# One word list for another: a linear-attention and ReLU² kernel with all of its engine orders, transfers and banks rewritten

## The chip, the cores and the metric

The kernel runs on one core of a Trainium2 chip. The metric is device microseconds of one execution; the median of three runs before the change is 180.9 us (180.63 to 181.43). Five engines work side by side: PE (matmuls; its weight loads are listed apart as PEld), DVE (vector), ACT (activations and copies), POOL (a second elementwise engine) and SP, which here issues every transfer. Each engine takes its own instructions strictly in the order in which the program gives them; between engines, semaphores make an instruction wait for what it reads, or for the buffer that it overwrites.

## The reference

Two stages, for 4 batches, 8 heads, 768 positions and 48 channels to a head:

```python
for t in range(S):                                  # attention, a state of 48x48 per head
    cur = einsum('bhd,bhe->bhde', u * k_t, v_t)
    y_t = einsum('bhd,bhde->bhe', r_t, state + cur)
    state = w_t[..., None] * state + einsum('bhd,bhe->bhde', k_t, v_t)
x = y.transpose(0, 2, 1, 3).reshape(3072, 384)      # tokens x (heads * channels)
out = (maximum(x @ w_in, 0) ** 2) @ w_out           # 384 -> 2048 -> 384
```

r, k, v and w are float32, 4.7 MB each; w_in and w_out 3.1 MB each; the output is 4.7 MB.

## The kernel before, in words

The 3072 tokens are cut into 12 **steps** of 256 tokens, three to a batch. A step of the attention is done in chunks: logarithms of w are summed with a matmul (`cum_`), their exponentials scale r and k (`rd_`), products of r and k give a masked score matrix (`p_`, masked by `pm_`), which times v gives `y_`; the state of the chunk before enters through `yc_`, and the state is carried on by `su_` (a matmul), `ts_` (its sum with the old state) and `sn_` (its decay, on POOL). The result (`ysb_`, which also adds `vq_`, the u term) is turned (`yt_` and `xt_` through PE in steps 0 to 5, `dyt_` by a transposing transfer in steps 6 to 11) and goes into the second stage: `m1_.s.g` is one of 8 groups of the first product of step s (six matmuls), `rl_` its ReLU, `sq_` the square of two groups, `m2_.s.c.q` a quarter of the second product of half a step (four matmuls), `os_` scales it into an output tile, `store` sends it out. r and k of steps 0 to 3 are turned on PE (`tr_`, copied by `rkt_`), those of steps 4 to 11 by transposing transfers (`dtr_`).

The order of all this is a **word list**, ORDER: 865 words, each one operation. A loop at the end of the kernel takes them one by one and emits their instructions, so each engine's program is the list read with the other engines' words left out. `ld.3.k` loads k of step 3, `ld.1.i` a quarter of w_in, `ld.1.o` one of w_out; `=V`, `=A`, `=G` puts an operation on DVE, ACT or POOL; `:0` to `:3`, `:m`, `:b` give the PSUM bank. `warm_.8.5` is eight matmuls on zeros whose result nobody reads, there to keep PE going. Nothing but this list decides what stands behind what.

Buffers tie words together as well: four buffers for each of the raw inputs w, k, r, v, four staging buffers for the two weights, two for most tiles of the attention, three of `gt` (the values between the two products), four of the output. A transfer on SP's queue that has to wait, for a tile or for a buffer, holds up every transfer after it in the list.

Of the kernel before, what the change touches and what calls it, by code (L numbers as in the profile page):

```python
# [27 lines left out]
qp_.2=G pm_.2.1 pm_.2.0 su_.2:1 rl_.1.1=V ts_.2.0=V ld.2.i m1_.0.0:2 m1_.1.3:1 cast.i.2=A y_.2:1 q_.2 yc_.2.0
sn_.2.0 yc_.2.1 rl_.1.3=A m1_.0.5:3 ld.3.i m1_.1.5:1 ld.3.w m1_.0.4:0 rl_.0.0=A rl_.0.5=V qs_.2=A rl_.1.5=A
cast.i.3=G m1_.1.7:3 ld.0.o m1_.1.4:1 vq_.2=V ysb_.2=V rl_.0.4=A rl_.1.7=A ww_.3=G cast.o.0=G m1_.0.7:2 yt_.2:3  # L30
ld.2.o m1_.0.6:0 lw_.3 cast.o.2=G cum_.3:1 xt_.2=V rl_.0.7=V ld.3.o m1_.2.4:3 rl_.0.6=V sq_.0.1=A ld.1.o
sq_.0.0=A rl_.1.4=A m1_.2.2:2 sq_.0.2=A m1_.1.6:0 m1_.2.7:1 ld.3.r rl_.1.6=A sq_.1.1=A rl_.2.2=V rl_.2.4=V
m1_.2.5:2 rl_.2.7=V ld.3.k al_.3 rl_.2.5=V cast.o.1=V m1_.2.6:0 m2_.0.1.0:3 m2_.0.1.2 sq_.1.3=V kw_.3=G
m1_.2.3:1 sq_.1.0=A ld.3.v ld.5.w m2_.0.0.0:2 ac_.3 ld.4.w ld.4.r sq_.0.3=A rl_.2.6=A exp_.3 vs_.3.1=G ld.4.v
ld.4.k m1_.2.0:0 m2_.0.0.2 m2_.0.1.1 cast.o.3=V rl_.2.0=A m1_.2.1:0 rw_.3=V m2_.0.1.3 sq_.2.3=A rl_.2.1=A
sq_.1.2=A rl_.2.3=A rd_.3.0 m2_.0.0.1 os_.0.1=A tr_.3.0:0 rd_.3.1 m2_.0.0.3 tr_.3.1:1 ku_.3=V m2_.1.0.1:3
os_.0.0=A m2_.1.0.0 rkt_.3.0=V rkt_.3.1=V p_.3.0:0 v_.3=G sq_.2.1=A su_.3:1 sq_.2.2=A vs_.3.0=A qp_.3=V ld.5.k
p_.3.1:b ts_.3.0=A m2_.2.0.1:2 m2_.1.0.3 m2_.2.0.3 m2_.1.0.2 sq_.2.0=A ww_.4=G pm_.3.0 lw_.4 q_.3 qs_.3=A
cum_.4:0 m2_.2.0.0 ld.6.w v_.4=A pm_.3.1 ww_.5=G rw_.4=G sn_.3.0 ts_.3.1=V vq_.3=G ac_.4 al_.4 m2_.2.0.2
yc_.3.1:1 y_.3 m2_.2.1.0:1 m2_.2.1.2 os_.1.0=A kw_.4=V lw_.5 ysb_.3=V sn_.3.1 store.0.0 os_.2.0=A exp_.4 kw_.5=G  # L40
rd_.4.1 rd_.4.0 cum_.5:1 ac_.5 yt_.3:3 vs_.4.1=G xt_.3=A ld.5.r vs_.4.0=A al_.5 store.0.1 ld.6.r m2_.2.1.3
m2_.2.1.1 os_.2.1=V m1_.3.0:3 rl_.3.0=A exp_.5 su_.4:0 m1_.3.1:2 rl_.3.1=A m2_.1.1.3:0 m2_.1.1.1 dtr_.4.1
ku_.4=V qp_.4=V rw_.5=V m1_.3.7:2 rl_.3.7=A m1_.3.6:1 ts_.4.0=V dtr_.4.0 rl_.3.6=A m2_.1.1.2 m1_.3.5:3 rd_.5.1
rl_.3.5=A m1_.3.4:1 sn_.4.0 ts_.4.1=V p_.4.0:0 q_.4 rd_.5.0 qs_.4=A ww_.6=G vq_.4=G rw_.6=G p_.4.1:1 sq_.3.0=V
m2_.3.1.0:3 m2_.1.1.0 pm_.4.0 yc_.4.1:0 yc_.4.0 sq_.3.3=A m1_.3.3:2 rl_.3.4=A sq_.3.2=A pm_.4.1 y_.4 lw_.6
m1_.3.2:1 rl_.3.3=A rl_.3.2=A cum_.6:1 m2_.3.0.2:2 m2_.3.0.3 sq_.3.1=A m2_.3.1.3 m2_.3.1.1 ku_.5=G qp_.5=G
ld.5.v ysb_.4=V al_.6 ld.7.w ld.6.k ww_.7=G yt_.4:1 m2_.3.1.2 m2_.3.0.0 exp_.6 ac_.6 os_.1.1=V sn_.4.1 m2_.3.0.1
kw_.6=V rd_.6.0 rd_.6.1 dtr_.5.1 ld.6.v v_.5=G dtr_.5.0 xt_.4=A p_.5.1:1 store.2.0 ld.7.r vs_.5.1=A os_.3.1=A
lw_.7 su_.5:b p_.5.0:0 q_.5 v_.6=A store.2.1 ts_.5.0=V m1_.4.1:1 ku_.6=G rl_.4.1=A vs_.6.0=A m1_.4.3:0 os_.3.0=A
pm_.5.0 pm_.5.1 rl_.4.3=V m1_.4.2:3 rl_.4.2=A vs_.6.1=A qs_.5=G m1_.4.4:1 sn_.5.0 yc_.5.1:0 yc_.5.0 rl_.4.4=V  # L50
su_.6:1 dtr_.6.0 m1_.4.7:3 rl_.4.7=A vs_.5.0=G dtr_.6.1 y_.5 m1_.4.6:1 ts_.6.0=V sn_.6.0 ld.9.w m1_.4.5:3
m1_.4.0:2 vq_.5=V sq_.4.1=A rl_.4.6=A rl_.4.5=A sq_.4.2=A ysb_.5=V ts_.6.1=V rl_.4.0=V sq_.4.0=V yt_.5:0
m2_.4.1.1:1 xt_.5=A qp_.6=G q_.6 qs_.6=G ld.7.k p_.6.0:1 ld.8.v yc_.6.1:0 ld.7.v ld.8.r p_.6.1:m store.1.1
ld.8.w vq_.6=G ku_.7=G pm_.6.1 sq_.4.3=A kw_.7=G m2_.4.1.0 m2_.4.1.2 m1_.5.1:0 rl_.5.1=A pm_.6.0 m2_.4.1.3
sn_.6.1 m1_.5.0:2 cum_.7:1 y_.6 m1_.5.7:3 vs_.7.0=A rl_.5.0=A os_.4.1=A ww_.9=V al_.7 m2_.4.0.0:0 rl_.5.7=V
m1_.5.2:2 m1_.5.6:1 ww_.8=G rw_.7=G exp_.7 ac_.7 m2_.4.0.1 vs_.7.1=G m2_.4.0.2 m1_.5.3:3 rl_.5.2=A sq_.5.0=A
v_.7=A rl_.5.3=A m1_.5.5:2 sq_.5.1=A ysb_.6=V vs_.8.0=G m2_.4.0.3 lw_.8 rl_.5.6=A rd_.7.1 qp_.7=V rd_.7.0
sq_.5.3=A su_.7:0 v_.8=G rl_.5.5=V rw_.8=V m1_.5.4:3 rl_.5.4=V m2_.5.1.0:2 cum_.8:1 sq_.5.2=A ts_.7.0=V al_.8
q_.7 m2_.5.1.1 m2_.5.1.3 store.1.0 ld.8.k ld.11.k ac_.8 store.3.1 dyt_.6 dtr_.7.1 dtr_.7.0 exp_.8 kw_.8=V
sn_.7.0 ts_.7.1=V m1_.6.2:3 m2_.5.1.2 m1_.6.3:1 ld.9.r ld.10.w sn_.7.1 os_.4.0=A rd_.8.1 m1_.6.1:0 os_.5.1=A  # L60
ku_.8=G m1_.6.7:2 rd_.8.0 rl_.6.2=V ld.9.k rl_.6.3=A qs_.7=A m1_.6.4:1 su_.8:1 rl_.6.7=A p_.7.1:m p_.7.0:0
qp_.8=G rl_.6.1=V ts_.8.0=V yc_.7.1:1 yc_.7.0 rl_.6.4=A sq_.6.1=A m2_.5.0.2:0 m1_.6.6:1 store.3.0 rl_.6.6=A
sq_.6.3=A dtr_.8.1 pm_.7.1 pm_.7.0 lw_.9 dtr_.8.0 m2_.5.0.1 m1_.6.5:2 y_.7 m1_.6.0:3 m2_.5.0.3 m2_.5.0.0
store.4.1 ku_.9=G q_.8 qs_.8=G ww_.10=G rl_.6.5=V vq_.7=V rl_.6.0=A vs_.8.1=A rw_.9=G sq_.6.0=A p_.8.0:m
p_.8.1:0 kw_.9=G qp_.9=G ysb_.7=V cum_.9:1 m2_.6.0.1:1 ld.9.v ld.10.k os_.5.0=A m2_.6.0.3 m2_.6.1.3:0 m2_.6.0.0
sq_.6.2=V m2_.6.0.2 m2_.6.1.0 sn_.8.0 al_.9 exp_.9 pm_.8.0 rd_.9.0 pm_.8.1 dyt_.7 v_.9=A ac_.9 m1_.7.7:2 y_.8:0
yc_.8.1 rd_.9.1 su_.9:1 vs_.9.1=A yc_.8.0 rl_.7.7=A m1_.7.4:3 ld.10.v vq_.8=G ysb_.8=V m1_.7.0:2 lw_.10
store.4.0 q_.9 rl_.7.4=A ts_.9.0=A rl_.7.0=A cum_.10:0 al_.10 vs_.9.0=V exp_.10 m2_.6.1.1 os_.6.0=V m2_.6.1.2
os_.6.1=A m1_.7.5:2 m1_.7.6:3 m1_.7.2:0 kw_.10=G ld.11.w dtr_.9.0 kw_.11=V qs_.9=G rl_.7.5=A ld.10.r dyt_.8
sq_.7.2=A m1_.7.3:2 m1_.7.1:1 rl_.7.6=A dtr_.9.1 m1_.8.5:3 rl_.7.3=A rl_.7.1=A m1_.8.6:2 v_.10=G sn_.9.0  # L70
ts_.9.1=V rw_.10=G rd_.10.1 rd_.10.0 ac_.10 ku_.11=G rl_.7.2=A rl_.8.5=V sq_.7.1=A ld.11.v m1_.8.7:1 p_.9.0:1
p_.9.1:0 m1_.8.1:3 ww_.11=G store.6.1 vq_.9=G ld.11.r vs_.10.1=G store.6.0 pm_.9.0 sn_.9.1 rl_.8.6=A rl_.8.7=A
rl_.8.1=A lw_.11 m2_.7.1.2:0 m2_.7.1.1 pm_.9.1 m1_.8.3:2 y_.9:0 yc_.9.1 su_.10:1 ysb_.9=V dtr_.10.0 m1_.8.4:1
sq_.7.3=A sq_.7.0=A cum_.11:0 m2_.7.1.3 m2_.7.1.0 ts_.10.0=V rw_.11=V rl_.8.4=A rl_.8.3=V dtr_.10.1 ku_.10=G
sq_.8.2=A os_.7.1=A m1_.8.0:1 m2_.7.0.0:3 m2_.8.1.2:2 m1_.8.2:0 m2_.7.0.1 m2_.7.0.3 m2_.7.0.2 al_.11 exp_.11
rd_.11.1 rd_.11.0 vs_.11.1=G v_.11=G ac_.11 rl_.8.0=A sq_.8.0=A yc_.10.0:0 rl_.8.2=V qp_.10=G p_.10.1:b sn_.10.0
vs_.10.0=G ts_.10.1=V q_.10 qs_.10=G store.7.1 dyt_.9 yc_.10.1 p_.10.0:1 m2_.8.1.0 pm_.10.0 qp_.11=G sn_.10.1
# [555 lines left out]
```

## Time and profile before

| what | value |
|---|---|
| median of 3 runs | 180.9 us |
| lowest, highest | 180.63, 181.43 us |
| profiled execution, first to last instruction (span) | 178.8 us |
| between that span and the median of the runs | 2.1 us |
| PE busy | 171.0 us, 96% of the span |
| DVE, ACT, POOL busy | 138.0, 133.4, 108.0 us |
| bytes moved by the transfers | 35.81 MB |
| first matmul of the second stage (`m1_`) | at 26.02 us |

The profile gives the profiled execution no time of its own beside its span, so what lies around the span is taken as the difference to the median, 2.1 us. Times in what follows are us from the start of the span. A busy time of PE counts matmuls from their start to their modelled end, and these overlap: rows of the chain of waits, which have starts that follow each other, tell more of PE's pace than a mean duration does.

### The profile page before, as it was taken

How to read it: one execution, taken by the hardware profiler on the slowest of the kernel's cores; microseconds unless marked ns; L12 is line 12 of the kernel's file. 1: busy time of each engine (PE TensorE's matmuls, PEld its weight loads, DVE VectorE, ACT ScalarE, POOL GpSimd, SP SyncE). 2: the span in 40 equal slices, each digit the busy share in tenths (PEclk: the TensorE clock that was granted, in tenths of full speed). 3: DMA queues.
4: the chain of work that ended last, by engine and by line, in shares of the span. 5: the costliest groups of instructions: out<-in, count | busy, mean ns of one | idle time of the engine just before them, and what ended most of it. 6: DMA issues, size and time to landing. Idle time of an engine off the chain costs nothing.

```text
span 178.8 us, 5697 instructions
## 1 busy us (share of the span) xinstructions
PE 171.0 (96%) x2383; PEld 123.9 (69%) x2385; DVE 138.0 (77%) x204; ACT 133.4 (75%) x238; POOL 108.0 (60%) x132
## 2 busy tenths in 40 slices
...
GB/s 144 268 263 252 259 346 361 344 368 260 266 243 237 191 216 185 290 166 259 273 291 151 213 255 224 222 175 245 226 79 148 55 48 40 127 12 88 88 44 88
DMA packets 78952, 35.81 MB, mean 200 GB/s; under 512 B 72144, under 2 KB 77392, under 8 KB 78928
## 3 DMA queue, kind: packets, MB, share of 16 engines
...
q8 instruction: 18, 0.29, 0.7%
...
## 4 chain that ended last, share of the span: by engine, by line
PE 56%; POOL 16%; DMA 10%; DVE 9%; issue 4%; SPq 3%; ACT 1%; POOLq 0%; ACTq 0%; DVEq 0%
PE m L562 16%; PE bk L534 11%; PE m L534 11%; PE bk L562 10%; DMA k_raw<-in_k_dram 7%; POOL ku L297 3%; DMA kT<-kdec_buf 3%; POOL r_raw L286 2%; SPq L178 2%; POOL ku L302 2%; DVE pmT L432 2%; PE att L418 2%; POOL ku L316 2%; POOL S L459 2%; DVE y_sb L502 2%
## 5 line engine op out<-in xcount | busy, mean ns | idle before, releaser
L534 PEld LDWEIGHTS <-wi_sb 128*128 128x128 bf16 x576 | 54.9, 98 | 10.7 <-ACT wi_sb L200 0.6
L562 PEld LDWEIGHTS <-gt 128*128 128x128 bf16 x384 | 36.7, 98 | 20.6
L534 PE MATMUL m<-xT,wi_sb 128*128 128x256 bf16 x306 | 40.2, 273 | 0.1
L551 ACT ACTIVATE gt<-gt 128x1024 bf16<-128x1024 f16 x37 | 38.1, 1051 | 0.5
L534 PE MATMUL bk<-xT,wi_sb 128*128 128x256 bf16 x270 | 35.8, 273 | 0.4 <-ACT wi_sb L200 0.4
L562 PE MATMUL bk<-wo_sb,gt 128*128 128x384 bf16 x192 | 35.6, 326 | 0.0
L562 PE MATMUL m<-wo_sb,gt 128*128 128x384 bf16 x192 | 35.0, 326 | 0.0
L543 ACT ACTIVATE gt<-m 128x512 f16<-128x512 f32 x33 | 19.4, 595 | 11.5 <-PE m L534 11.2
L543 ACT ACTIVATE gt<-bk 128x512 f16<-128x512 f32 x35 | 20.6, 596 | 7.2 <-PE bk L534 6.9
L545 DVE TENSOR_SCALAR gt<-m 128x512 f16<-128x512 f32 x18 | 12.3, 688 | 13.1 <-PE m L534 12.4
L432 DVE TENSOR_TENSOR pmT<-att,mask 128x1024 bf16<-128x1024 f32 x16 | 19.1, 1218 | 1.9 <-PE att L418 1.8
L316 POOL TENSOR_TENSOR ku<-v_sh,qs 128x768 f32<-128x768 bf16 x9 | 13.3, 1475 | 10.6 <-ACT qs L277 10.5
L459 POOL TENSOR_TENSOR S<-t_state,ac_buf 128x192 bf16<-128x192 f32 x20 | 12.2, 610 | 8.2 <-DVE t_state L454 5.5
L297 POOL TENSOR_TENSOR ku<-k_raw,u_bc 128x768 f32<-128x768 f32 x9 | 16.7, 1854 | 0.2 <-DMA k_raw<-in_k_dram 0.2
L502 DVE TENSOR_TENSOR y_sb<-att,ku 128x768 bf16<-128x768 f32 x12 | 11.5, 955 | 4.4 <-POOL ku L316 2.0
L290 POOL TENSOR_TENSOR k_raw<-k_raw,w_raw 128x384 f32<-128x384 f32 x8 | 8.1, 1012 | 10.9 <-DMA k_raw<-in_k_dram 10.9
L361 DVE TENSOR_TENSOR kdec_buf<-k_raw,att 128x768 bf16<-128x768 f32 x12 | 11.4, 950 | 3.7 <-ACT att L340 3.7
L277 ACT CAST v_sh<-v_raw 64x384 bf16<-64x384 f32 x26 | 13.2, 509 | 0.3
L302 POOL TENSOR_TENSOR ku<-ku,r_raw 128x768 f32<-128x768 f32 x7 | 12.7, 1811 | 0.2
L358 DVE TENSOR_TENSOR rdec_buf<-r_raw,att 128x384 bf16<-128x384 f32 x24 | 12.3, 547 | 0.6 <-POOL r_raw L286 0.4
L277 POOL CAST v_sh<-v_raw 64x384 bf16<-64x384 f32 x18 | 10.0, 556 | 3.3 <-DMA v_raw<-in_v_dram 2.0
L307 DVE TENSOR_REDUCE q<-ku 128x16 f32<-128x768 f32 x12 | 11.3, 944 | 0.0
...
## 6 DMA issues: line engine op xcount, KB each, us to landing
...
```

Source lines behind the costliest of these rows:

```text
L277: copy(out[j * Q:(j + 1) * Q, c], src[c * Q:(c + 1) * Q, :, j])
L297: tensor_mul("ku_", s, h)(tiles["ku", s][:, hs], raw["k", s][:, hs, 1:3, :], u_bc[:, hs, None, :].to_broadcast([C, n, 2, D]))
L302: tensor_mul("qp_", s, h)(ku, ku, raw["r", s][:, heads(h), 0:2, :])
L316: tensor_mul("vq_", s)(vq[:], tiles["vs", s][:], tiles["qs", s][:, :, :, None].to_broadcast([C, 2, H, D]))
L358: nc.vector.tensor_mul(rdec[0][:, ps, j, :, 0:D], x[:, :, j, :].rearrange("p (a e) d -> p a e d", e=2), dec.rearrange("p (a e) d -> p a e ...
L432: nc.vector.tensor_mul(pmT, ps_p[:].rearrange("p e (x t) -> p (e x) t", t=C), mk.to_broadcast([C, 8, C]))
L459: nc.gpsimd.tensor_mul(t[:], tiles.pop(("ts", s, c))[:].rearrange("p (a d) -> p a d", a=HP), tiles["a_c", s][:, :, c, None].to_broadcast([ ...
L502: nc.vector.tensor_add(tiles["ysb", s][:, x].rearrange("p c (a e d) -> p (c a) e d", e=2, d=D), tiles["y", s][:, :, cols].rearrange("p e ( ...
L534: nc.tensor.matmul(ps1[:, j, :], wi_sb[:, n // 4, kk, n % 4 * 128:(n % 4 + 1) * 128], tiles["xT", s][:, :, kk, :], start=(kk == 0), stop=( ...
L543: nc.scalar.activation(rl, m1, AF.Relu, scale=RS)
L551: nc.scalar.activation(gt, rl, AF.Square)
L562: nc.tensor.matmul(m2, gt[:, 4 * q + n, c * C:(c + 1) * C], wo_sb[:, 4 * q + n, :], start=(summed[s, c] == 1 and n == 0), stop=(summed[s, ...
```

## The change

The word list is replaced. Both lists have 865 words, and the same 865 operations when engines and banks are left out; the 46 warming matmuls are dealt out differently. Changed are the order on every engine and on SP's queue, 122 of the choices of an engine, and 102 of the 194 choices of a PSUM bank. By engine: POOL has one `cast`, one `kw_`, one `qp_`, three `rw_` and two `vs_` more, and two `ww_`, two `v_` and one `vq_` fewer; DVE has four `rl_`, five `sq_`, three `xt_`, two `ww_`, one `os_` and one `vq_` more and three `rw_`, one `kw_`, one `qp_`, one `cast`, one `vs_` and one `rkt_` fewer; ACT has four `rl_`, five `sq_`, three `xt_`, one `os_` and one `vs_` fewer and two `v_` and one `rkt_` more. `warm_` takes a third argument that it doesn't use.

```diff
 ORDER = """
-ld.0.w ld.0.k ld.0.r ld.0.u ld.1.w ww_.0=V lw_.0 warm_.11.5 cum_.0:0 kw_.0=G exp_.0 rd_.0.1 ld.0.v warm_.8.5
-tr_.0.1:0 rkt_.0.1=A ld.1.k ld.1.r rw_.0=G ld.2.w ku_.0=G rd_.0.0 ld.1.v warm_.3.5 tr_.0.0:1 ww_.1=V rkt_.0.0=A
-qp_.0=V ld.2.r v_.0=A warm_.5.5 p_.0.0:m p_.0.1:1 ac_.0 lw_.1 q_.0 su_.0:b ld.2.k cum_.1:0 ts_.0.0=A kw_.1=G
-pm_.0.0 pm_.0.1 vs_.0.0=A sn_.0.0 ld.1.i exp_.1 rw_.1=G vs_.0.1=A qs_.0=A warm_.3.2 ku_.1=G rd_.1.0 rd_.1.1
-warm_.2.2 ts_.0.1=V qp_.1=V warm_.4.2 ld.0.i tr_.1.0:0 rkt_.1.0=V tr_.1.1:2 ac_.1 sn_.0.1 q_.1 ww_.2=G
-rkt_.1.1=A vs_.1.0=A lw_.2 v_.1=G y_.0:0 yc_.0.1 p_.1.1:1 p_.1.0:m warm_.6.1 vq_.0=G pm_.1.1 cum_.2:1 vs_.1.1=A
-pm_.1.0 qs_.1=A exp_.2 warm_.4.1 su_.1:m kw_.2=G ysb_.0=V rw_.2=G ts_.1.0=V y_.1:0 rd_.2.1 yc_.1.0 rd_.2.0
-yt_.0:1 xt_.0=V sn_.1.0 cast.i.1=A vq_.1=G ts_.1.1=V tr_.2.1:2 yc_.1.1 ld.2.v tr_.2.0:0 m1_.0.3:1 rkt_.2.1=A
...
-os_.11.1=V m2_.11.0.1 store.10.0 store.9.0 store.10.1 m2_.11.0.0 m2_.11.0.3 store.11.1 os_.11.0=A store.11.0
+ld.0.w warm_.11.4.0 ld.0.k ld.0.r ld.0.u ld.1.w ww_.0=V ld.0.v lw_.0 cum_.0:1 ld.1.k kw_.0=V warm_.4.0.8 exp_.0
+warm_.8.3.1 rd_.0.1 rw_.0=G rd_.0.0 ld.1.r tr_.0.1:3 ku_.0=V tr_.0.0:0 rkt_.0.1=A ld.1.v warm_.3.2.4 ww_.1=V
+warm_.2.1.5 rkt_.0.0=A qp_.0=V warm_.5.3.3 ld.2.k ac_.0 q_.0 vs_.0.1=A v_.0=G p_.0.0:m pm_.0.0 vs_.0.0=G su_.0:b lw_.1
+ld.2.w warm_.3.4.2 ts_.0.0=A sn_.0.0 kw_.1=V p_.0.1:0 cum_.1:1 ld.2.r pm_.0.1 warm_.6.3.7 exp_.1 rw_.1=G ac_.1 rd_.1.0
+qs_.0=A ku_.1=G yc_.0.1:0 y_.0 rd_.1.1 tr_.1.0:3 ld.1.i v_.1=A ts_.0.1=V tr_.1.1:0 qp_.1=V rkt_.1.0=A sn_.0.1 ld.0.i
+ld.2.v q_.1 rkt_.1.1=A su_.1:m ld.2.i ts_.1.0=V vs_.1.1=A p_.1.0:1 ww_.2=G p_.1.1:b pm_.1.0 ld.3.i vq_.0=G lw_.2
+vs_.1.0=A pm_.1.1 cum_.2:1 warm_.4.2.6 kw_.2=G exp_.2 ysb_.0=V ld.3.k qs_.1=A rw_.2=G rd_.2.1 yt_.0:1 y_.1:0 ac_.2
+cast.i.1=A sn_.1.0 rd_.2.0 tr_.2.1:2 vq_.1=G yc_.1.0 yc_.1.1 xt_.0=V tr_.2.0:0 rkt_.2.1=A ts_.1.1=V ld.3.w m1_.0.3:1
...
+store.5.1 m1_.6.6:2 rl_.6.0=A sn_.8.0 ld.9.v m2_.5.0.2:3 vs_.8.0=G rl_.6.5=A rl_.6.6=V sq_.6.1=A y_.7 m2_.5.0.0
+kw_.9=G ysb_.7=V sq_.6.0=A m2_.5.0.1 ku_.9=G vq_.8=V dyt_.7 sq_.6.2=A p_.8.1:b p_.8.0:1 yc_.8.0:0 yc_.8.1 pm_.8.0
+m2_.6.0.0:2 sq_.6.3=A store.4.1 ld.10.k cum_.9:1 m2_.6.0.2 pm_.8.1 ld.10.v v_.9=A rw_.9=G m2_.5.0.3 al_.9 y_.8 qp_.9=G
...
+os_.11.0=V m2_.10.0.2 store.11.0 m2_.11.1.1 m2_.10.0.0 os_.11.1=V m2_.10.0.3 store.11.1 os_.10.0=A store.10.0
 """
...
-    def warm_(n, i):
+    def warm_(n, i, x=0):
```

The first rows are both lists up to the first `m1_`; the later ones are a place around `y_.8` and the two ends.

More of the change, by code (lines that the diff above doesn't have):

```diff
@@ L28 @@
[L28 to L77, printed above, removed]
```

71 lines of the change are left out of this document (57 added, 14 removed).

## The prediction

> **What bounds the kernel now.** I read the page first, then PE's stretches, then the chain of waits, and last the opening on each engine.
>
> ```profile
> span 178.8 us, 5697 instructions
> PE 171.0 (96%) x2383; PEld 123.9 (69%) x2385; DVE 138.0 (77%) x204; ACT 133.4 (75%) x238; POOL 108.0 (60%) x132
> ...
> 26.02:175.02 149.00, 148.60 (x2058) 111.70 (x2059) 117.43 (x169) 115.51 (x202) 88.66 (x103) 1.00 0.84 194
> ```
>
> The stretch row gives length, then busy time of PE, PEld, DVE, ACT and POOL, granted clock (1.00: full), DMA share and GB/s. From 26.02 on PE is busy 148.60 of 149.00 us; before that it partly warms. So there are three stages: the **opening** to the first `m1_`, the **dense stage**, and a **tail** (last matmul, `os_`, store). The lists hold the same matmuls, so only three things can move: when `m1_` starts, what PE loses between matmuls, and the tail. The chain of waits has the prices of the dense stage (start, duration, what):
>
> ```profile
> 39.27 1.31 PE m L534 x12
> 43.20 1.30 PE m L562 x8
> 50.82 0.45 PE bk L374 x8
> 52.56 0.36 PE att L418 x16
> 52.92 0.26 PE att L444 x32
> 53.18 0.28 PE bk L418 x16
> 53.47 2.71 PE m L562 x16
> 62.34 0.37 PE att L444 x32
> 62.71 0.76 PE m L534 x6
> 68.04 0.58 PE att L418 x32
> 68.62 0.76 PE m L562 x4
> 70.03 0.37 PE att L491 x32
> 70.40 0.76 PE m L534 x6
> 71.16 0.40 PE att L481 x16
> 72.22 0.08 PE att L324 x4
> 72.29 0.18 PE att L326
> 75.09 0.33 PE bk L514 x6
> 173.46 1.96 PE bk L562 x12
> 175.50 0.49 ACT o_sb L569
> ```
>
> An `m1_` word (six matmuls, L534) takes 1.31/2 = 0.655 us, an `m2_` word (four, L562) 1.30/2 = 0.65. Going into the 64-row matmuls (`p_` L418, `su_` L444, `yc_` L491) and out costs extra: `su_` alone takes 0.37, and the `m1_` behind it 0.76 in place of 0.66, so 0.47; two `p_` alone 0.58 + 0.11 = 0.69; `p_ su_ p_` in one visit 0.36 + 0.26 + 0.28 + 0.11 = 1.01, not 1.16. **One visit thus costs about 0.15**, beside 0.27 for a `p_`, 0.32 for a `su_` and, from 0.37 + 0.10 less a visit for two, 0.16 for a `yc_`. `y_` is 0.40, `cum_` 0.26, `yt_` 0.33, `tr_` 0.45.
>
> Sum of the dense stage before: 96 x 0.655 + 96 x 0.65 + 20 `p_` x 0.27 + 10 `su_` x 0.32 + 17 `yc_` x 0.16 + 10 `y_` x 0.40 + 9 `cum_` x 0.26 + 5 `yt_` x 0.33 + 2 `tr_` x 0.45 + 20 visits x 0.15 = 148.4 us. From 26.02 to 173.46 + 1.96 = 175.42 are 149.4. **All waits of PE in this stage are worth 1.0 us.** That is nearly all that better orders can win there.
>
> **The change, part by part.**
>
> *Dense stage, same words.* All words ahead of the first `m1_` on PE are the same set in both lists (`cum_` 0 to 2, `tr_` 0 to 2, `p_`, `su_`, `y_` of steps 0 and 1, three `yc_`, `yt_.0`, 46 warming matmuls). So the dense stage holds the same work. Reading the lists PE word by PE word, the 64-row words form 20 visits before and 17 after: 3 x 0.15 = **-0.45 us**. Bounds: 0, if the dearer `m1_` behind a visit has another cause, to -0.6 at 0.20 a visit (0.69 + 0.47 - 1.01 with all roundings one way).
>
> *Opening.* What sets the first `m1_`:
>
> ```profile
> 6.25 1.00 POOL L290 TENSOR_TENSOR k_raw<-k_raw,w_raw 128x384 f32<-128x384 f32 x1 [2.60 <-DMA k_raw<-in_k_dram]
> 13.10 1.02 POOL L290 TENSOR_TENSOR k_raw<-k_raw,w_raw 128x384 f32<-128x384 f32 x1 [2.73 <-DMA k_raw<-in_k_dram]
> 17.34 1.33 POOL L459 TENSOR_TENSOR S<-t_state,ac_buf 128x192 bf16<-128x192 f32 x1
> 20.37 1.47 POOL L316 TENSOR_TENSOR ku<-v_sh,qs 128x768 f32<-128x768 bf16 x1
> 23.73 0.51 POOL L459 TENSOR_TENSOR S<-t_state,ac_buf 128x192 bf16<-128x192 f32 x1
> 4.63 0.56 DVE L264 TENSOR_TENSOR ww<-w_raw 128x384 f32<-128x384 f32 x1 [0.97 <-DMA w_raw<-in_w_dram]
> 7.66 0.95 DVE L361 TENSOR_TENSOR kdec_buf<-k_raw,att 128x768 bf16<-128x768 f32 x1 [2.47 <-ACT att L340]
> 9.99 0.80 DVE L264 TENSOR_TENSOR ww<-w_raw 128x384 f32<-128x384 f32 x1 [0.45 <-DMA w_raw<-in_w_dram]
> 17.35 0.96 DVE L302 TENSOR_TENSOR ku<-ku,r_raw 128x768 f32<-128x768 f32 x1
> 18.22 0.68 DVE L389 COPY rT<-bk 128x1024 bf16<-128x1024 bf16 x1
> 24.93 0.55 DVE L519 COPY xT<-bk 128x768 bf16<-128x768 bf16 x1
> 24.50 1.47 ACT L200 CAST wi_sb<-w_st 128x1536 bf16<-128x1536 f32 x1 [1.57 <-DMA w_st<-in_moe_w_in_dram]
> 26.02 0.83 PE L534 MATMUL bk<-xT,wi_sb 128*128 128x256 bf16 x6 [0.39 <-ACT wi_sb L200]
> ```
>
> Two things meet at 26.02: `cast.i.1`, which waits for its load (24.50 + 1.47 = 25.97), and `xt_.0` on DVE (done at 25.48). *The load:* `ld.1.i` is the 13th transfer in both lists, behind the same twelve. Loads follow each other: from the second (6.25) to the seventh (13.10) are 4.5 full loads, since u has half a load's bytes, so 1.52 us each. Five more and a weight load of twice the bytes would land it at 13.10 + 7 x 1.52 = 23.7; it landed at 24.5. Some 0.8 us were lost on the way, and the list does not change what is ahead. I keep 24.5; the lower bound is 23.7.
>
> The page has this row on instruction fetches:
>
> ```profile
> q8 instruction: 18, 0.29, 0.7%
> ```
>
> That is 16 KB each. [...]
>
> *DVE's queue ahead of `xt_.0`:* it gains `kw_.0`, `ku_.0` and `kw_.1` and loses `rkt_.1.0`. `kw_.0` has the shape of the 0.56 row and fits into the 2.47 us in which DVE waits for the exponential. `ku_.0` (shape of the 0.96 row) and `kw_.1` (0.56) less 0.68 leave +0.84. The 0.45 of idle time at 9.99 takes up part: `xt_.0` done at 25.48 + 0.84 - 0.45 = 25.9. *POOL's queue ahead of it:* `ld.2.w` moves from the 9th place to the 11th, so it lands four loads after 13.10, at 19.2 (20.0 with the lost 0.8); `ww_.2`, `vq_.0`, `kw_.2`, `rw_.2` (1.02 for the three of 128x384 as at 13.10, 1.47 for `vq_`) end at 23.7 to 24.5, and `rd_.2.0` (about 1.0, as its sister's 0.95 at 7.66) and `xt_.0` (0.55) behind them at 25.2 to 26.1. So cast, DVE and POOL all arrive near 26. Bounds of the first `m1_`: 25.2 (no lost time, no collision) to 27.3 (a `sn_` took 1.33 beside DVE's `qp_.1` at 17.35 and 0.51 alone: two such collisions). I take 26.3, **+0.3**: any one of the three being late is enough.
>
> *Waits in the dense stage.* Some places of the new list have no room. Between `y_.7` and `y_.8` the new list puts five `m2_`, two `p_`, two `yc_`, one visit and one `cum_`, 4.5 us of PE; DVE must do `ysb_.7`, `vq_.8` and both `pm_.8` in it:
>
> ```profile
> L502 DVE TENSOR_TENSOR y_sb<-att,ku 128x768 bf16<-128x768 f32 x12 | 11.5, 955 | 4.4 <-POOL ku L316 2.0 <-POOL S L459 1.3 <-PE att L481 0.8
> L432 DVE TENSOR_TENSOR pmT<-att,mask 128x1024 bf16<-128x1024 f32 x16 | 19.1, 1218 | 1.9 <-PE att L418 1.8
> L429 DVE TENSOR_TENSOR pmT<-m,mask 128x512 bf16<-128x512 f32 x12 | 7.7, 682 | 0.2 <-PE m L418 0.2
> ```
>
> 0.96 + 0.96 (the 128x768 product at 17.35) + 1.22 + 2 x 0.68 = 4.5 us: cover and cost are equal, and what is late next is `y_.8`, then all of PE behind it. I take the same 1.0 us of waits as before, **0**; bounds -1.0 (none left) and +2.0 (POOL, below).
>
> *Tail.* Both lists end with the last `m2_`, an `os_` on ACT (0.49) and its store: **0**.
>
> Sum: 178.8 - 0.45 + 0.3 + 0 + 0 = 178.65; with the 2.1 us that lie between this span and the median of 180.9, **180.8 us**. What a measurement of this kernel can tell from no change is about 0.5%, 0.9 us.
>
> **The rivals.**
>
> *No waits left (faster).* The new order loses nothing on PE, and the load comes as in the stream without loss. -0.45 - 1.0 = -1.45 with `m1_` at 26.0: **179.4**, down to 178.6 with `m1_` at 25.2. For: no sum above forces any wait, only collisions do. Against: a dense stage that loses 1.0 us in 149 is near its floor already.
>
> *POOL becomes the bound (slower).* Between PE's 40 and 120 us the old list used POOL like this:
>
> ```profile
> 40.00:120.00 80.00, 79.92 (x1197) 59.05 (x1195) 74.69 (x108) 69.47 (x124) 57.14 (x68) 1.00 1.04 229
> ```
>
> 57.1 us for 68 instructions, 0.84 each. Adding up PE's prices along the new list, 64 POOL words with 84 instructions fall in this stretch: 70.6 us of 80 at that mean. Above 95% (76 us) every collision is passed on: POOL's decayed states (`sn_`) and `vq_` come late, and PE stands at `yc_` and behind `ysb_`. It decides from a mean of 0.905 us an instruction on. Half of the collision seen at 17.34 (0.8) at five such places is +2.0: **182.7**. For: the mean holds only if the mix does not grow dearer, and seven `ku_` and six `qp_` are in it. Against: POOL waited a good part of the old stretch.
>
> [...]
>
> *The opening loses (slower).* Two collisions on DVE's longer queue put `m1_` at 27.3: 180.9 - 0.45 + 1.3 = **181.8**. Against: POOL has `kw_.0` and `ku_.0` less there.
>
> **How the numbers follow.** My forecast (180.8, its own range 180.1 to 181.7) 0.40; no waits left 0.29; POOL 0.19; the opening 0.12, of which a third stays within 0.9 us. Faster by over 0.5% is 0.29, within it 0.40 + 0.04 = 0.44, slower 0.27. The range goes from 178.9 (most of the faster case) to 183.0 (past POOL's price).
>
> **What would show it.** Right: first `m1_` at 26.0 to 26.6, the dense stage at 148.5 to 149.5, `y_.8` with a wait below 0.3. POOL's rival: PE waits at `yc_` or `y_` whose releaser is `S` or `ku` on POOL, POOL above 76 us between 40 and 120. The opening's: `xt_.0` ends after 26.8 behind DVE instructions longer than 0.56 and 0.96. I am wrong altogether if the load of `ld.1.i` lands before 23 or after 26, or if PE waits for transposing transfers (`dtr_`, `dyt_`).

## The result, and the profile after

The changed kernel takes **188.2 us** (187.1 to 188.8 over four runs) against 181.1 for the kernel before beside it: a ratio of 1.039 (1.035 to 1.044). It is slower by 7.1 us, outside the range of the prediction. The profiled execution is the shortest of the four, 187.1 us with a span of 185.3. Line numbers of the new kernel are four lower than before's: `m1_` is L530, `m2_` L558, `p_` L414, `cum_` L320 and L322.

The first lines of the page of the kernel after (span; busy time, share and count of each engine):

```profile
span 185.3 us, 5699 instructions
PE 171.6 (93%) x2382; PEld 123.7 (67%) x2385; DVE 144.8 (78%) x212; ACT 125.0 (67%) x226; POOL 113.0 (61%) x137
```

Two rows of its stretches, from the first `m1_` on and the one in which the prediction weighed POOL (length; busy time of PE, PEld, DVE, ACT and POOL; clock, DMA share, GB/s):

```profile
26.68:182.00 155.32, 149.54 (x2062) 111.72 (x2059) 123.27 (x176) 107.16 (x190) 96.83 (x110) 1.00 0.82 186
40.00:120.00 80.00, 76.17 (x1141) 56.41 (x1139) 70.36 (x101) 61.32 (x107) 68.32 (x77) 1.00 1.04 231
```

PE does the same work, 171.6 us against 171.0, in a span that is 6.5 us longer. The dense stage takes 155.3 us where it took 149.4. By the prediction's prices (148.4 - 0.45) it holds 147.95 us of words, so **its waits are worth 7.4 us, not 1.0**. That, and an opening 0.7 us later, less the 0.45 for the visits, is the whole loss (6.4 + 0.7 - 0.45 = 6.65, against 6.5 of span). These parts come out of one subtraction, so they must add up; the waits themselves can be seen in the rows of waits of PE and PEld in the kernel after (us, times, longest). Those of PE behind the first `m1_` sum to some 5.6 us; before, the same view lists none behind the 0.4 us at 26.02:

```profile
PE att L320 <- DVE pmT L425: 1.7, 1, 1.7
PE att L320 <- DVE pmT L428: 1.3, 1, 1.3
PE bk L530 <- ACT gt L539: 1.2, 1, 1.2
PE att L414 <- DMA kT<-kdec_buf: 1.2, 1, 1.2
...
PE m L530 <- DVE xT L515: 0.5, 1, 0.5
...
PE m L414 <- ACT gt L539: 0.4, 1, 0.4
...
PEld L414 <- DMA kT<-kdec_buf: 1.9, 2, 1.5
```

The row on L425 is ahead of the dense stage. The others are chains through two or three queues. Three of them in the timeline of the kernel after (start, duration, engine, line, what; in brackets the idle time ahead of it) are shown here.

**At 80 us: a transposing transfer.** `p_.5.0` waits for `dtr_.5.1` (L397, kT):

```profile
57.95 2.13 SPq L174 DMA_DIRECT2D k_raw<-in_k_dram  x1
64.26 1.33 SPq L394 DMA_TRANSPOSE rT<-rdec_buf  x1
...
71.91 4.27 SPq L397 DMA_TRANSPOSE kT<-kdec_buf  x1
80.05 0.65 PE L414 MATMUL att<-rT,kT 64*64 64x128 bf16 x32 [1.20 <-DMA kT<-kdec_buf]
```

The chain of waits has the transfer from its issue to its landing:

```profile
71.91 8.10 DMA kT<-kdec_buf
```

SP issues nothing from 57.95 + 2.13 = 60.08 to 64.26: at its head stands `dtr_.4.0`, which needs `rd_.4.0`. Three loads behind it (`ld.6.v`, `ld.5.v`, `ld.7.k`) could have gone. They go later, ahead of `dtr_.5.1`, which is issued at 71.91 and lands 8.10 us after that, at 80.0. Standing still is not a loss by itself: the kernel before stood still at its first transposing transfer almost as long, from 56.15 + 0.43 = 56.58 to 60.53, and no wait of PE came of it. There only three loads stand between the transfers of step 4 and `dtr_.5.1`. Its rows (kernel before):

```profile
56.15 0.43 SPq L178 DMA_DIRECT2D r_raw<-in_r_dram  x1
60.53 1.32 SPq L401 DMA_TRANSPOSE kT<-kdec_buf  x1
```

**At 116 us: products that DVE and POOL make at the same time.** `cum_.9` takes the bank in which `p_.8.0` stood, so it waits until `pm_.8.0` (DVE L428) has read it:

```profile
112.08 1.83 POOL L293 TENSOR_TENSOR ku<-k_raw,u_bc 128x768 f32<-128x768 f32 x1
113.86 1.72 POOL L282 TENSOR_TENSOR r_raw<-r_raw,w_raw 128x384 f32<-128x384 f32 x1
112.94 1.78 DVE L312 TENSOR_TENSOR ku<-v_sh,qs 128x768 f32<-128x768 bf16 x1
114.65 1.21 DVE L428 TENSOR_TENSOR pmT<-att,mask 128x1024 bf16<-128x1024 f32 x1
115.91 0.24 PE L320 MATMUL att<-half_ones,lw_buf 128*128 128x2 bf16 x4 [1.30 <-DVE pmT L428]
117.31 0.99 POOL L282 TENSOR_TENSOR r_raw<-r_raw,w_raw 128x384 f32<-128x384 f32 x1
```

`vq_.8` on DVE (L312) takes 1.78 and ends 0.81 after POOL's `ku_.9` has ended at 113.91; POOL's next product takes 1.72 where its twin at 117.31 takes 0.99. The rows look as if each had waited for the other. The same happens at 39 us: `ku_.3` on DVE takes 1.68, and the first `m1_` of step 2 waits 0.5 us for `xt_.2` behind it. Where POOL makes nothing beside it, as in the kernel locks further below, the same `ku_.3` takes 0.95 (POOL idle for 2.96 us there):

```profile
41.36 0.95 DVE L293 TENSOR_TENSOR ku<-k_raw,u_bc 128x768 f32<-128x768 f32 x1
```

**At 127 us: a load, four queues away.**

```profile
122.21 0.82 POOL L268 CAST v_bf<-v_raw 128x768 bf16<-128x768 f32 x1 [3.91 <-PE m L558]
123.00 1.00 POOL L286 TENSOR_TENSOR k_raw<-k_raw,w_raw 128x384 f32<-128x384 f32 x1
126.01 0.18 ACT L342 ACTIVATE ac_buf<-att 128x8 f32<-128x8 f32 x1 [2.28 <-DVE rdec_buf L354]
126.08 0.59 ACT L539 ACTIVATE gt<-bk 128x512 f16<-128x512 f32 x1
126.72 0.82 PE L530 MATMUL bk<-xT,wi_sb 128*128 128x256 bf16 x6 [1.23 <-ACT gt L539]
```

Read from below: `m1_.7.3` waits for the bank that `rl_.7.4` on ACT frees; that stands behind `ac_.10`, which in this order stands behind `rd_.10.0` on DVE; that needs `kw_.10` (POOL, 123.00), which stands behind `v_.10` (122.21). The profile puts POOL's 3.91 us of idle time down to a matmul, but the load that `v_.10` reads was issued at 115.49, and the list of issues between 114 and 124 us (count, size, us from issue to landing) has it landing 6.6 us later, at 122.1:

```profile
v_raw<-in_v_dram SPq DMA_DIRECT2D x1, 384.0 KB, 6.6
```

The matmul named, of `m2_`, reads `wo_sb` and `gt`, which the cast neither reads nor writes, so its wait is put down here to the load, which lands 0.1 us before the cast begins; in e_v10, further below, the profile itself names this load ahead of the same cast, which begins at 122.98 there. The 0.4 us ahead of `p_.9.1`, at 129 us, stand behind the same late queue of ACT.

The opening: first `m1_` at 26.70 by the timeline, behind `cast.i.1` and `xt_.0`, which end together. Rows of POOL (`ww_.2`), ACT (`ac_.2`, then the cast) and DVE (`xt_.0`):

```profile
20.54 0.99 POOL L260 TENSOR_TENSOR ww<-w_raw 128x384 f32<-128x384 f32 x1 [1.02 <-DMA w_raw<-in_w_dram]
24.95 0.18 ACT L342 ACTIVATE ac_buf<-att 128x8 f32<-128x8 f32 x1 [0.41 <-DVE kdec_buf L357]
25.16 1.47 ACT L196 CAST wi_sb<-w_st 128x1536 bf16<-128x1536 f32 x1
26.10 0.55 DVE L515 COPY xT<-bk 128x768 bf16<-128x768 bf16 x1
```

### The profile page after: what moved, and what is told of

The parts are those of the page before. It is cut to its first block, busy times and chain, and to the rows that moved or that the text cites. A ratio compares the mean times of both kernels' runs of the same rounds, so it can differ in the third digit from the quotient of the medians.

```text
span 185.3 us, 5699 instructions
## 1 busy us (share of the span) xinstructions
PE 171.6 (93%) x2382; PEld 123.7 (67%) x2385; DVE 144.8 (78%) x212; ACT 125.0 (67%) x226; POOL 113.0 (61%) x137
## 4 chain that ended last, share of the span: by engine, by line
PE 52%; DVE 13%; DMA 4%; ACT 4%; issue 2%; DVEq 0%; ACTq 0%
PE bk L558 13%; PE bk L530 12%; PE m L558 11%; PE m L530 10%; DMA kT<-kdec_buf 4%; DVE gt L549 2%; PE att L477 2%; ACT gt L547 2%; DVE gt L541 1%; DVE pmT L428 1%; PE att L414 1%; ACT gt L539 1%; DVE rdec_buf L354 1%; DVE pmT L425 1%; DVE kdec_buf L357 1%
## 5 line engine op out<-in xcount | busy, mean ns | idle before, releaser
L530 PEld LDWEIGHTS <-wi_sb 128*128 128x128 bf16 x576 | 55.2, 98 | 12.5 <-issue 2.9
L558 PEld LDWEIGHTS <-gt 128*128 128x128 bf16 x384 | 36.3, 98 | 21.4 <-ACT gt L547 0.6
L530 PE MATMUL bk<-xT,wi_sb 128*128 128x256 bf16 x306 | 40.0, 273 | 1.2 <-ACT gt L539 1.2
L558 PE MATMUL m<-wo_sb,gt 128*128 128x384 bf16 x208 | 39.2, 327 | 0.2 <-ACT gt L547 0.2
L530 PE MATMUL m<-xT,wi_sb 128*128 128x256 bf16 x270 | 35.7, 273 | 0.9 <-DVE xT L515 0.5
L558 PE MATMUL bk<-wo_sb,gt 128*128 128x384 bf16 x176 | 33.4, 327 | 0.5 <-DVE gt L549 0.2
L547 ACT ACTIVATE gt<-gt 128x1024 bf16<-128x1024 f16 x32 | 33.1, 1054 | 0.6 <-DVE gt L541 0.2
L539 ACT ACTIVATE gt<-m 128x512 f16<-128x512 f32 x29 | 17.0, 593 | 11.5 <-PE m L530 8.9
L428 DVE TENSOR_TENSOR pmT<-att,mask 128x1024 bf16<-128x1024 f32 x15 | 18.2, 1216 | 2.0 <-PE att L414 2.0
L549 DVE TENSOR_TENSOR gt<-gt 128x1024 bf16<-128x1024 f16 x16 | 13.6, 873 | 6.0 <-ACT gt L539 5.9
L312 POOL TENSOR_TENSOR ku<-v_sh,qs 128x768 f32<-128x768 bf16 x8 | 12.1, 1517 | 5.9 <-ACT qs L273 3.8
L282 POOL TENSOR_TENSOR r_raw<-r_raw,w_raw 128x384 f32<-128x384 f32 x11 | 12.7, 1157 | 4.8 <-DMA r_raw<-in_r_dram 4.6
L565 ACT ACTIVATE o_sb<-bk 128x384 f32<-128x384 f32 x9 | 4.4, 490 | 16.4 <-PE bk L558 13.4
L273 POOL CAST v_sh<-v_raw 64x384 bf16<-64x384 f32 x22 | 12.5, 570 | 2.7 <-DMA v_raw<-in_v_dram 1.8
```

Source lines behind the costliest of these rows:

```text
L273: copy(out[j * Q:(j + 1) * Q, c], src[c * Q:(c + 1) * Q, :, j])
L282: tensor_mul("rw_", s, h)(raw["r", s][:, hs, 2, :], raw["r", s][:, hs, 1, :], raw["w", s][:, hs, 0, :])
L428: nc.vector.tensor_mul(pmT, ps_p[:].rearrange("p e (x t) -> p (e x) t", t=C), mk.to_broadcast([C, 8, C]))
L530: nc.tensor.matmul(ps1[:, j, :], wi_sb[:, n // 4, kk, n % 4 * 128:(n % 4 + 1) * 128], tiles["xT", s][:, :, kk, :], start=(kk == 0), stop=( ...
L539: nc.scalar.activation(rl, m1, AF.Relu, scale=RS)
L547: nc.scalar.activation(gt, rl, AF.Square)
```

## The experiments

Two theories went in. **Transfers**: data come late, because loads stand behind transposing transfers that wait for an engine. **Places in queues**: transfers and products are in time or could be, but single instructions stand where they hold up others. Words below are given for one engine's queue alone. All ratios are to the kernel before on the same chip, which took 180.8 to 181.2 us.

### Single chains cut, and three together

```diff
 # c_dtr5: SP
 dtr_.5.0 store.2.1
+dtr_.5.1
 ld.6.v ld.5.v store.1.0 ld.7.k
-dtr_.5.1
 # e_v10: POOL
 rw_.10
+kw_.10
 v_.10
-kw_.10
 # d_vq8: vq_.8 on POOL (vs_.8.0, vq_.8, kw_.9) in place of DVE (ysb_.7, vq_.8, pm_.8.0)
 # cde: all three
```

> dtr_.5.1 moves four places forward on SP's queue, ahead of ld.6.v, ld.5.v, store.1.0 and ld.7.k. In the changed kernel PE stood 1.5 us at 80.04 before p_.5 until this transfer had landed (80.00). If the queue of transfers makes that wait: it lands near 72, PE has no wait at p_.5, and the time falls by 1.0 to 1.3 us, from 188.2 to about 187. If the stage is late as a whole (the engines behind, so that the next wait takes it over): within 0.3 us of 188.2, with the waits at 116 and 127 grown by what this one lost.

> On POOL v_.10 moves behind kw_.10, nothing else. In the changed kernel v_.10 waited for ld.10.v until 122.2, kw_.10 stood behind it, rd_.10 on DVE behind that, ac_.10 on ACT behind rd_.10, rl_.7.4 behind ac_.10, and m1_.7.3 on PE for the bank of rl_.7.4 (about 1.4 us at 127). If this chain from one late load through four queues is the cause: 1.4 to 1.9 us less, about 186.5. If PE is late there for DVE's or ACT's own load: within 0.4 us of 188.2.

> vq_.8 moves from DVE to POOL, ahead of kw_.9. In the changed kernel it took 1.78 us on DVE beside ku_.9 on POOL, 0.83 more than alone; both pm_.8 stood behind it and cum_.9 on PE waited 1.6 us at 116 for the bank of pm_.8.0. If the shut-out and DVE's queue make that wait: cum_.9 goes 1.0 to 1.3 us earlier, about 187.1. If POOL is the bound there (it has no idle time from 97 to 118): its 1.5 us more come back as a wait for rw_.9 or sn_, and the time stays at 188.2 or rises.

> The three edits together. If each removes a wait of its own and nothing behind takes it over: their gains add, 3.4 to 4.5 us less than 188.2, 183.8 to 184.8. If PE's waits are a common lateness: less than 2 us in all, with new waits in other places.

| kernel | us (lowest to highest) | ratio |
|---|---|---|
| after | 188.2 (187.1 to 188.8) | 1.039 (1.035 to 1.044) |
| c_dtr5 | 188.4 (187.8 to 188.8) | 1.038 (1.034 to 1.043) |
| e_v10 | 187.4 (187.1 to 187.6) | 1.033 (1.029 to 1.037) |
| d_vq8 | 187.4 (186.8 to 187.9) | 1.032 (1.027 to 1.037) |
| cde | 187.1 (185.9 to 187.7) | 1.031 (1.026 to 1.036) |

Each kernel ran beside runs of its own of the kernel before, so gains against the kernel after are best read from the ratios. Those of e_v10, d_vq8 and cde overlap with its interval: gains of 0.8 us are at the edge of what these runs can tell. c_dtr5 came as its second theory said (no gain), e_v10 between its two, d_vq8 near its first, cde as its second said (under 2 us). What the expectation of d_vq8 calls the shut-out is the 0.83 us by which `vq_.8` was longer than alone (1.78 against 0.95 to 0.96 for the three other `vq_` on DVE in the kernel after); no run shows what makes it.

Each cut takes away the wait that it aims at (all but 0.3 us of it in d_vq8), and other waits take its place. In c_dtr5 `p_.5.0` no longer waits, but `ld.5.v` and the transposed r of step 6, pushed back, now come late: ACT's `vs_.5.1` waits for the first, `ac_.6` behind it frees its bank late, and PE waits (waits of PE in c_dtr5):

```profile
PE att L414 <- ACT ac_buf L342: 0.9, 1, 0.9
PE m L414 <- DMA rT<-rdec_buf: 0.6, 1, 0.6
```

The three together give 1.1 us where the three waits sum to 3.7 in the rows above. So a chain that is cut shows the next one that is nearly as late.

### SP's queue alone

```diff
 # sp_first: SP
 ld.6.w ld.5.k
+ld.6.v ld.5.v ld.7.k
 dtr_.4.0 dtr_.4.1 dtr_.5.0 store.2.1
-ld.6.v ld.5.v
 store.1.0
-ld.7.k
 dtr_.5.1
 # sp_early: that, and also
 store.4.0
+ld.9.v ld.10.k ld.10.v
 dtr_.8.0 dtr_.8.1 store.5.1 dyt_.7 store.4.1
+ld.11.w ld.11.k ld.11.v
 dyt_.8
```

> The kernel after, with SP's queue alone changed: ld.6.v, ld.5.v and ld.7.k stand ahead of dtr_.4.0, ld.9.v, ld.10.k and ld.10.v ahead of dtr_.8.0, and ld.11.w, ld.11.k and ld.11.v ahead of dyt_.8, so that no load stands behind a transfer that waits for an engine. Theory of the transfers (what is late in the new order is the data, because loads stand behind waiting transposing transfers): the waits ahead of p_.5 (1.1 to 1.4 us), at 127 us (1.4) and ahead of p_.9 (0.5) go, and the time is 185.2 us, 184.5 to 186. Theory of the engines' queues (the loads would be in time if the instruction that needs them stood later in its own queue, and other lateness takes over when one wait is removed): within 0.7 us of the 188.2 of the kernel after.

> The kernel after, with only the first of the three moves on SP's queue: ld.6.v, ld.5.v and ld.7.k ahead of dtr_.4.0, in the stretch where SP stands still for 4 us at dtr_.4.0; dtr_.8.0 and dyt_.8 keep their places. If the transfers are one nearly full stream, and a move pays only where SP would have stood still: the wait ahead of p_.5 (1.1 us) goes, no wait of over 1 us comes in at p_.8, and the time is 187.0 us, 186.5 to 187.5. If moving loads ahead of transposing transfers is a loss anywhere: above 188.5, with PE waiting at p_.4 or p_.5.

sp_early took **190.1 us** (189.9 to 190.3), ratio 1.050 (1.048 to 1.053): neither theory's time. sp_first took **186.5 us** (186.2 to 186.8), ratio 1.031 (1.028 to 1.034), as expected there. In both, the wait at `p_.5` is gone (the row of sp_first has no idle time ahead of it):

```profile
78.97 0.65 PE L414 MATMUL att<-rT,kT 64*64 64x128 bf16 x32
```

SP no longer stands still. The stretch from 60 to 66 us of sp_first has a DMA share of 0.81 and 197 GB/s (the last two numbers), where the kernel after had 0.59 and 135:

```profile
60.00:66.00 6.00, 5.76 (x46) 4.30 (x45) 4.88 (x9) 5.52 (x11) 5.83 (x8) 1.00 0.81 197
```

But ahead of `dtr_.8.0` SP stood still for 1.8 us only (105.50 to 107.33 in the kernel after). There three loads put ahead of it push `dtr_.8` back, by more than PE's slack (sp_early, PE, then SP):

```profile
116.94 0.65 PE L414 MATMUL bk<-rT,kT 64*64 64x128 bf16 x16 [4.45 <-DMA kT<-kdec_buf]
...
107.04 1.61 SPq L174 DMA_DIRECT2D v_raw<-in_v_dram  x1
108.76 3.81 SPq L394 DMA_TRANSPOSE rT<-rdec_buf  x1
112.62 1.54 SPq L397 DMA_TRANSPOSE kT<-kdec_buf  x1
```

In the kernel after, `dtr_.8.1` is issued at 108.62; here at 112.62, and PE waits 4.45 us. Of these 4.0 us, 1.4 are the later issue of `dtr_.8.0` (107.33 there, 108.76 here), and 2.6 its longer hold of SP (1.23 there, 3.81 here). So the theory of transfers holds in this form: the stream is nearly full (a DMA share of 1.04 between 40 and 120 us, before and after), and loads put ahead of a transposing transfer gained where SP had stood still for 4.2 us (sp_first) and lost where it had stood still for 1.8 (the later moves of sp_early, which make 190.1 out of 186.5).

### SP's order of after on the engines of before

> The kernel before, all its engines as they were, with SP's queue in the order of the kernel after (but ld.7.w ahead of dtr_.6.1 and ld.9.w ahead of dyt_.6, as its POOL needs them). Theory of the transfers: it loses what the kernel after loses at them, about 3 us, 184 us, 183 to 186. Theory of the engines' queues: the queues of before leave room for late data (v_.10 stands behind kw_.10), so that it stays within 1 us of the 181.1 of before.

It took **204.4 us** (204.2 to 205.4), ratio 1.130 (1.126 to 1.134): +23 us, far past both theories. SP stands still for up to 8.3 us (from 93.98 + 2.13 to 104.38) at a transposing transfer whose data need loads and engines that are late already, and everything behind it waits too:

```profile
93.98 2.13 SPq L174 DMA_DIRECT2D w_raw<-in_w_dram  x1
104.38 1.22 SPq L519 DMA_TRANSPOSE xT<-y_sb  x1
```

An order of transfers thus has no price of its own. It fits one order of the engines, and with another it costs three times what the whole change cost.

### Products moved apart, and all of it together

locks moves `ku_.3` two places back on DVE and puts `ww_.5` and `vq_.8` on POOL. mended is locks, sp_early, e_v10, and two places on ACT (`sq_.1.1` ahead of `os_.2.1`, `vs_.11.1` behind `sq_.8.0`). mended2 is the same with sp_first in place of sp_early, and `ku_.3` one place further back. mended3 and mended4 go on from mended2:

```diff
 # mended4: DVE                       # mended3: behind rl_.2.0; POOL's own order is as in mended2
+rl_.2.7
 ku_.3
-rl_.2.7
 ...
 qp_.4
+os_.1.0
 q_.4
-os_.1.0
 # mended4: ACT
 sq_.8.2
+rl_.8.6
 ac_.11
+v_.11
 os_.7.0
-v_.11 rl_.8.6
 # mended3 also, PE: cum_.9 behind m2_.6.0.2 and m2_.5.0.3
```

> The kernel after, with three products moved so that two operations on two SBUF inputs no longer stand beside each other on DVE and POOL: ku_.3 behind rl_.0.7 on DVE, ww_.5 on POOL ahead of vq_.3, vq_.8 on POOL ahead of kw_.9. Theory of the collisions (the long instructions of 1.3 to 1.8 us on DVE are what PE waits for): the waits at 41 us (0.6), at 54 to 56 us (0.6) and at 116 us (1.5) go, and the time is 186.0 us, 185.5 to 186.5. If those waits are only where a common lateness shows: 187.2 to 188.2, no better than vq_.8 alone.

> The kernel after, with both of these, and v_.10 behind kw_.10 on POOL, sq_.1.1 ahead of os_.2.1 on ACT, vs_.11.1 behind sq_.8.0 on ACT. If the waits are separate mishaps, each with its own cause, they go together: 188.2 less about 6, 182 us, 181.5 to 183. If they are one lateness that shows at another place each time, 186 to 187.5, as with the three single edits together (187.1).

> The kernel after, with that first move on SP, ku_.3 behind rl_.1.6 on DVE, ww_.5 and vq_.8 on POOL, v_.10 behind kw_.10, sq_.1.1 ahead of os_.2.1 and vs_.11.1 behind sq_.8.0 on ACT. If PE's waits are separate mishaps, each with a place in a queue as its cause: some 3.5 us of waits are left in the dense stage, 184.1 us, 183.5 to 185. If one lateness shows at another place each time: 186.5 to 188.

> The kernel of mended2 with its four largest remaining waits treated singly: ku_.3 and qp_.3 behind rl_.2.0 (DVE, POOL), os_.1.0 ahead of q_.4 on DVE, cum_.9 behind m2_.5.0.3 on PE, rl_.8.6 ahead of ac_.11 and os_.7.0 behind v_.11 on ACT. If the waits are separate mishaps: 185.4 less 0.66, 0.55, 0.53 and 0.92, 182.7 us, 182 to 183.3. If the rest is one lateness of the whole order that shows at another place: 184.8 to 186.

> The kernel of mended2 with three of its remaining waits treated, and more gently than in mended3, where qp_.3, moved with ku_.3, held the cast of the first output weights on POOL for 1.8 us: ku_.3 one place later on DVE, behind rl_.2.7; os_.1.0 ahead of q_.4; rl_.8.6 ahead of ac_.11 and os_.7.0 behind v_.11. If the waits are single mishaps: 185.4 less 0.66, 0.55 and 0.92, 183.3 us, 182.5 to 184.2. If one lateness shows elsewhere: 184.8 to 186.

| kernel | us (lowest to highest) | ratio |
|---|---|---|
| locks | 186.9 (186.2 to 187.1) | 1.032 (1.029 to 1.035) |
| mended | 189.4 (188.6 to 190.4) | 1.045 (1.040 to 1.050) |
| mended2 | 185.4 (184.0 to 186.1) | 1.024 (1.019 to 1.028) |
| mended3 | 185.7 (185.1 to 186.7) | 1.026 (1.020 to 1.032) |
| mended4 | 184.5 (184.1 to 185.4) | 1.021 (1.016 to 1.025) |

locks came between its two theories (and its interval touches that of the kernel after). mended carries sp_early's long wait at `p_.8` and says little. mended2 gains 2.8 us, between the two theories and nearer to separate mishaps: nine moved words take away some 40% of the loss. mended4 gains 3.7 us, about half of it, again between its two theories; its runs overlap with those of mended2, so the step from one to the other is not clear of noise. mended3 shows what stands in the way of the rest. It put `ku_.3` later on DVE, and POOL's `qp_.3`, which reads it, held the cast of the first output weights; PE then waited for those (POOL, then PE):

```profile
44.35 1.80 POOL L298 TENSOR_TENSOR ku<-ku,r_raw 128x768 f32<-128x768 f32 x1 [4.75 <-DVE ku L293]
46.10 2.87 POOL L196 CAST wo_sb<-w_st 128x1536 bf16<-128x1536 f32 x2
47.62 0.81 PE L558 MATMUL m<-wo_sb,gt 128*128 128x384 bf16 x4 [1.76 <-POOL wo_sb L196]
```

mended3 also got a new wait of 1.4 us for a transposing transfer (of y, ahead of step 7), and its time is where the theory of one lateness put it. In mended4 the row at 47.62 is still 0.6 us late. Whether the other half of the loss is made of single places too, or is a lateness that no small move can take away, these runs do not settle.

### The price of a visit

b_visits, b_visits8 and b_visits5 are the kernel before with visits to the 64-row matmuls split by a neighbouring word, nine, eight and five of them:

```diff
 # b_visits5: PE (one of five)
 yc_.10.0 p_.10.1 yc_.10.1
+m2_.8.1.0
 p_.10.0
-m2_.8.1.0
 m1_.9.4
```

> The kernel before, with nine visits to the 64-row matmuls split in two by a neighbouring word of PE (between p_.4.0 and p_.4.1, yc_.4.1 and yc_.4.0, su_.5 and p_.5.0, yc_.5.0 and su_.6, yc_.7.1 and yc_.7.0, p_.8.0 and p_.8.1, p_.9.0 and p_.9.1, yc_.11.1 and p_.11.1, yc_.10.1 and p_.10.0). If a visit costs 0.15 us: 181.1 + 9 x 0.15 = 182.4 us. If it costs nothing: 181.1.

> The kernel before, with eight visits split as in b_visits but without the split between yc_.11.1 and p_.11.1, in which m1_.9.3 overwrote its bank ahead of the reader rl_.9.1. By the rows of b_visits a visit costs 0.22 to 0.25 us: 180.9 + 8 x 0.24 = 182.8 us if nothing else is late; by the 0.15 of the prediction 182.1. Waits of some microseconds beside them (as the 6 us in b_visits) would say that PE words moved by one place are enough to make the other queues late: 184 to 187.

> The kernel before, with five visits split in two: between su_.5 and p_.5.0, yc_.5.0 and su_.6, yc_.7.1 and yc_.7.0, p_.9.0 and p_.9.1, yc_.10.1 and p_.10.0. No bank is written ahead of its reader here. In its rows each split costs 0.22 to 0.25 us if a visit has that price, 0.15 by the prediction. Time: 180.9 + 5 x 0.24 = 182.1 us and at most 0.5 more for waits ahead of yc_.7.0 and p_.9.0; by the prediction's price 181.6.

In b_visits and b_visits8 the words overwrite a bank ahead of its reader (`m1_.9.3` ahead of `rl_.9.1` in the first, and in both `cum_.9`, moved ahead of `p_.8.1`, ahead of `ysb_.7`), so part of the output is made of other sums; their times, 187.6 and 188.1 us, hold 6 us of waits and are not used. b_visits5 has clean banks: 182.6 us (182.3 to 184.5), ratio 1.012 (1.006 to 1.017). One of its splits, before (first fence) and in b_visits5:

```profile
136.23 0.31 PE L491 MATMUL att<-S,rT 64*64 64x48 bf16 x16
...
136.73 0.40 PE L418 MATMUL att<-rT,kT 64*64 64x128 bf16 x16
137.06 0.82 PE L562 MATMUL m<-wo_sb,gt 128*128 128x384 bf16 x4
...
138.37 0.33 PE L562 MATMUL m<-wo_sb,gt 128*128 128x384 bf16 x1
```

```profile
137.61 0.31 PE L487 MATMUL att<-S,rT 64*64 64x48 bf16 x16
...
138.21 0.82 PE L558 MATMUL m<-wo_sb,gt 128*128 128x384 bf16 x4
138.96 0.43 PE L414 MATMUL att<-rT,kT 64*64 64x128 bf16 x16
...
139.98 0.81 PE L558 MATMUL m<-wo_sb,gt 128*128 128x384 bf16 x4
```

The same words take 138.37 - 136.23 = 2.14 and 139.98 - 137.61 = 2.37 us: **0.23 for one visit**. The other four splits, read in the same way, give 0.22 to 0.23. Five visits make 1.1 of the 1.8 us by which b_visits5 is slower. The rest is waits, 0.5 of it in `y_.10` for `pm_.10`: PE words moved by one place already cost some.

### The load of the first weights

```diff
 # b_early_i: SP of before
 ld.1.v ld.2.r
+ld.1.i
 ld.2.k
-ld.1.i
 ld.0.i
```

> The kernel before, with ld.1.i one place earlier in SP's queue, ahead of ld.2.k. If the load of the weights sets the first m1_ and xt_.0 stands 0.5 us behind it: the first m1_ at 25.5 to 25.6 in place of 26.02, 180.6 us. If it is held up by what is late through ld.2.k (kw_.2, and with it xt_.0): 181 to 182.

181.9 us (181.6 to 182.2), ratio 1.005 (1.003 to 1.008): slower, as the second case said. The weights came 2.2 us earlier, but `ld.2.k` later. POOL's `kw_.2` waited for it, and the first `m1_` came at 27.2 in place of 26.02:

```profile
23.78 1.01 POOL L286 TENSOR_TENSOR k_raw<-k_raw,w_raw 128x384 f32<-128x384 f32 x1 [1.88 <-DMA k_raw<-in_k_dram]
```

None of the kernels is faster than the kernel before.

## Why the prediction was wrong

- **The step that failed** is the waits in the dense stage: "the same 1.0 us of waits as before, 0; bounds -1.0 and +2.0". Measured: 7.4 us, +6.4. The sum took the new order's waits from the old order's, and its upper bound from POOL alone. The walk through the queues that the prediction made for the opening was not made for the dense stage, and SP's queue was not walked past `ld.1.i` at all. By the trace, 2.8 us of PE's waits hang on transfers: those at 80 us (1.2), at 127 us (1.2) and, behind the same late queue of ACT, ahead of `p_.9.1` (0.4). Another 2.0 us stand behind products that DVE makes beside POOL: `ku_.3` at 39 us (0.5), `ww_.5` at 52 us (0.2; it takes 1.33 where 0.56 is usual) and `vq_.8` at 113 us (1.3). That the products are long because of POOL is read from the rows and from `ku_.3` in locks; the edits that moved `vq_.8` and `ww_.5` also made DVE's queue shorter, so they do not tell the two apart. The working of the prediction's sum is not what failed: its terms add to 148.5 in place of 148.4, which makes the waits 0.9 and 7.3.
- **`y_.8`, the place named as having no room**, was the right place and the wrong size: the sum of DVE was 4.5 us with `vq_.8` at 0.96; it took 1.78, and PE lost 1.3 us at `cum_.9`, which stands ahead of `y_.8` and waits for the same chain. The prediction found cover and cost equal and still took 0. A sum with no margin should have been given a loss.
- **Visits**: -0.45 at 0.15 each. b_visits5 says 0.23, so three fewer would be worth -0.7, a little past the lower bound of -0.6. Of no weight here.
- **Opening**: +0.3 forecast, +0.7 measured, within its bounds, and by one of the three paths given, POOL's. The load of `ld.1.i` landed at 24.4 and did not set the start: the cast began at 25.16, behind `ac_.2`, which waited for DVE. DVE was late through POOL: `ww_.2` waited for `ld.2.w` and began at 20.54, where the prediction had that load land at 19.2 to 20.0, and `vq_.0` behind it ended at 22.96, on which `ysb_.0` on DVE waited. The cast and `xt_.0` ended within 0.05 us of each other at 26.6.
- **Tail**: 0 forecast; right (the last `os_` takes 0.49 in both).
- **The rivals.** POOL as the bound did not come: POOL was busy for 68.3 us between 40 and 120, where the prediction set 76, 95% of the stretch, as the point from which it decides (a choice of the prediction's that no run tests), and no long wait of PE has `S` or `ku` on POOL as its releaser. It is not wholly out, though: from 97 to 118 us POOL was busy for 20.47 of 21.00 us, and the collision at 113 us stands there. And the collisions that it priced at "five such places", +2.0, did occur, at three places that PE waits for, 2.0 us in all, without POOL being full over the stage. What makes these products long no row names. The rows at 112 to 115 us look as if each of the two had begun when the other ended: `vq_.8` ends 0.81 us after `ku_.9`, and `rw_.9` 0.86 us after `vq_.8`. Products of DVE that read a PSUM bank were not longer there beside POOL: `ysb_.7` took 0.96 at 112.07, as all twelve `ysb_` did (0.94 to 0.96), and `pm_.8.0` 1.21 at 114.65, where the mean of its form is 1.22. The condition "if PE waits for transposing transfers" is the one that came true.
- **What was not weighed** is that both directions are open for each wait: c_dtr5, sp_early and mended3 show an edit that removes a wait and makes others as large or larger two queues away. The forecast "like before" for an order with every place changed had nothing in the profile to rest on: before loses 1.0 us in 149, and b_spA shows that the same engines lose 23 with another order of their transfers.
